# Attention with an expert layer behind it on one core: two count copies removed, a scale moved to VectorE, a subtraction to GpSimd, and one pair's V maxima at other places

## The chip, the core and the metric

The kernel runs on one core of a Trainium2 chip. The metric is the time of one execution in microseconds (us). The engines are TensorE (PE; its weight loads are PEld), VectorE (DVE), ScalarE (ACT), GpSimd (POOL) and SyncE (SP, which issues DMAs). Each engine works through its own instructions in the order in which they stand.

## What is computed

The inputs are q, k and v of 8 batches, 8 heads, 1152 positions and 64 columns. Pairs of neighbouring queries are averaged, so that there are 576 queries a head; attention follows, and the 4608 rows of 512 that come out go to the one of 8 experts that a router picks for each:

```python
q_pool = q.reshape(B, H, S // factor, factor, D).mean(axis=3)
attn = softmax(scale * q_pool @ k^T)
x = (attn @ v).transpose(0, 2, 1, 3).reshape(B * S, H * D)
e_idx = argmax(x @ w_gate)
...
h = relu(x[mask] @ w1[e]); ye = h @ w2[e]
out[mask] = gate_w[mask] * sigmoid(x @ w_output_gate)[mask, e] * ye
```

## The kernel before

**Attention** goes through 32 pairs (batch, two heads) in an order that is written out by hand. The program counts steps, 18 to a pair (one for each of 9 key blocks of each head) and 3 places to a step. In each step TensorE makes the scores of one block (L392 and L394, tile `sps`), one or two row maxima groups of the next pair (L329, tile `mp`), and sums of probabilities by V of a pair before (L421 to L423, tile `av`). VectorE takes the maxima (`pm`, L330). ScalarE makes two exponentials of a score block; the low part `pl` of the probabilities is their difference, made on VectorE where the block's number stands in `PLP` (L402, it reads the score's own PSUM buffer and sets it free) and on GpSimd for the others (L408). There are two score buffers, used in turn, so the scores of an odd block wait for L402 of the odd block before. When a head's sums are done, VectorE sets the `av` buffer free with three instructions (`r`, `r`, `xb`, L430 to L432).

**Preparation of a pair** is a table of places (`PREPF` for the first pair, `PREP0` for the second, `PREP` for the others): loads, casts, splits, and at the end V. V is scaled by a power of two from its largest absolute value: ScalarE makes the maxima (`amax`, L266, tiles `junk` and `am`), TensorE adds them up over the partitions (`gmax`, L271), VectorE cuts the exponent out of PSUM into `ex` (`scale` 0, L276), GpSimd clamps and multiplies `ex` to `inv` (`scale` 1, L279, 128 x 2 elements), VectorE takes the reciprocal `sc` (`scale` 2, L281). Then V's high half is made on ScalarE (`vh`, L284, tile `vt`) and its low half on GpSimd (`vs`, L288, and `vl`, L291). Inside attention TensorE, VectorE, ScalarE and GpSimd follow the written order.

**The router** behind each batch's last pair counts rows by expert in `cum` (bf16, L582) and scatters row numbers by DMAs that GpSimd issues (L587). Once, in the sixth batch, `setup` copies `cum` into `cb1` (L757) and adds it up over the partitions by a matmul (L761) to pick an early expert.

**The expert layer** (`run`) loads that expert's weights, splits the first one into a rounded half `w1h` on ScalarE (L865) and the rest `w1l` on VectorE (L866) while the last pair's attention still runs, and goes through tiles of 256 rows (`l1`, L901 to L911, `l2`, L923 to L925). Before the first tile `totals1` copies `cum` into `cb` (L940), a matmul adds it up into `cp` (L942), and `totals2` and `totals3` make the tables of tiles on VectorE (L947 to L1023).

Of the kernel before, what the change touches and what calls it, by code (L numbers as in the profile page):

```python
# [8 lines left out]
F32 = mybir.dt.float32  # L9
F32R = mybir.dt.float32r  # L10
F16 = mybir.dt.float16
BF16 = mybir.dt.bfloat16
# [3 lines left out]
ALU = mybir.AluOpType  # L16
# [8 lines left out]
        (53, 'lv'), (71, 'amax', 0), (74, 'amax', 1), (81, 'gmax'), (82, 'scale', 0), (85, 'scale', 1), (90, 'scale', 2), (93, 'vh', 0), (93, 'vs', 0), (96, 'vh', 1), (97, 'vl', 0), (100, 'vs', 1), (104, 'vl', 1))  # L25
PREPF = ((0, 'lf'), (1, 'fsel'), (3, 'qsv'), (4, 'kh', 0), (5, 'kh', 1), (6, 'klh', 0), (7, 'klh', 1), (8, 'sk', 0, 0), (9, 'sq0'), (10, 'sk', 0, 1), (11, 'sl', 0, 0), (13, 'qd'),
         (45, 'sl', 0, 1), (46, 'sk', 1, 0), (48, 'sk', 1, 1), (51, 'sq1'), (54, 'sl', 1, 0), (57, 'sl', 1, 1), (56, 'lv'),
         (78, 'amax', 0), (82, 'amax', 1), (88, 'gmax'), (89, 'scale', 0), (92, 'scale', 1), (95, 'scale', 2), (97, 'vh', 0), (97, 'vs', 0), (100, 'vh', 1), (101, 'vl', 0), (103, 'vs', 1), (107, 'vl', 1))
PREP = ((0, 'lk'), (12, 'kh', 0), (12, 'qsum'), (17, 'kh', 1), (18, 'kl'), (18, 'dk', 0), (19, 'dk', 1), (22, 'qh'), (24, 'dq', 0), (25, 'dq', 1), (26, 'ql'), (29, 'qd'), (30, 'dl', 0), (32, 'dl', 1),
        (63, 'lv'), (82, 'amax', 0), (88, 'amax', 1), (93, 'gmax'), (94, 'scale', 0), (95, 'scale', 1), (99, 'scale', 2), (100, 'vh', 0), (101, 'vs', 0), (103, 'vl', 0), (107, 'vh', 1), (107, 'vs', 1), (110, 'vl', 1))  # L30
BURST = {0: 2, 2: 2, 4: 2, 6: 2, 8: 1, 10: 2, 12: 2, 14: 2, 16: 3}
# [31 lines left out]


def attention(tc, qT, kT, vL, wg, keep, xrows, idscr, cum, pairs, setup, scat, init):
    nc = tc.nc
    nb = len(pairs) // 4
    with ExitStack() as ctx:
# [27 lines left out]
        def free(k):  # L96
            held.discard(k)
            banks.remove(k)
            banks.append(k)
# [5 lines left out]
        order = [(LASTN - 2) % 3, (LASTN - 1) % 3, LASTN % 3]  # L105
# [21 lines left out]
        def prep(n, table):  # L127
# [6 lines left out]
            kp = ld.tile([128, S], F32R, name=f"kp{n}", tag="kp", bufs=KPB)  # L134
# [9 lines left out]
            ex = sm.tile([128, 2], U32, name="ex")  # L144
            inv2 = sm.tile([128, 2], F32, name="inv2")
# [128 lines left out]
            def scale(i):  # L274
                if i == 0:
                    nc.vector.tensor_scalar(out=ex, in0=gm[0].bitcast(U32), scalar1=0x7F800000, scalar2=None, op0=ALU.bitwise_and)  # L276
                    free(gm[1])
                elif i == 1:
                    nc.gpsimd.tensor_scalar(out=inv2, in0=ex.bitcast(F32), scalar1=2.0 ** -100, scalar2=2.0 ** 3, op0=ALU.max, op1=ALU.mult)  # L279
                else:  # L280
                    nc.vector.reciprocal(out=sc, in_=inv2)  # L281

# [9 lines left out]

            P = functools.partial
            fns = dict(lf=lf, fsel=fsel, qsv=qsv, klh=klh, sk=sk, sl=sl, sq0=sq0, sq1=sq1, qd=qd, lk=lk, lv=lv, kh=kh, kl=kl, qsum=qsum, qh=qh, ql=ql, dk=dk, dq=dq, dl=dl, amax=amax, gmax=gmax, scale=scale, vh=vh, vs=vs, vl=vl)
            out = {}
            for r, name, *arg in table:
# [149 lines left out]
        ones = keep['ones']  # L446
# [57 lines left out]
        def router(b, xb):  # L504
# [90 lines left out]
            if b == max(nb - 3, 0):  # L595
                yield from setup(psum, free)
# [112 lines left out]
class Moe:  # L709
# [38 lines left out]
    def setup(self, psum, free):  # L748

        nc, kp, k, P1 = self.tc.nc, self.kp, self.keep, self.P1  # L750
        V = nc.vector
        if not P1:
            V.memset(k['oh1'], 0.0)
            V.memset(k['ef'][:, 0:2], 0.0)
            return
        cb = kp.tile([128, 8], BF16, name="cb1")
        V.tensor_copy(out=cb, in_=self.cum)  # L757
        yield
        yield 1
        cp, ck = psum(True)  # L760
        nc.tensor.matmul(cp[:, 0:8], lhsT=k['ones'], rhs=cb, start=True, stop=True)  # L761
        em = k['em8'][:, 0]
        cn, eq, mx, mi = cp[:, 0:8], cp[:, 8:16], cp[:, 16:17], cp[:, 17:18]
        V.tensor_reduce(out=mx, in_=cn, axis=AX.X, op=ALU.max)
        yield
        ms = kp.tile([128, 1], F32, name="mx1")
        V.tensor_copy(out=ms, in_=mx)
        V.tensor_tensor(out=eq, in0=cn, in1=ms.broadcast_to([128, 8]), op=ALU.is_equal)
        yield
        V.tensor_tensor(out=eq, in0=eq, in1=em, op=ALU.mult)  # L770
        V.tensor_reduce(out=mi, in_=eq, axis=AX.X, op=ALU.min)
        yield
        V.tensor_scalar(out=k['ef'][:, 1:2], in0=mi, scalar1=8.0, scalar2=None, op0=ALU.add)
        V.tensor_tensor(out=k['oh1'], in0=em, in1=mi.broadcast_to([128, 8]), op=ALU.is_equal)
        V.memset(k['ef'][:, 0:1], 0.0)
        yield
        V.tensor_scalar(out=k['es'], in0=mi, scalar1=8.0, scalar2=None, op0=ALU.add)
        ri = kp.tile([128, 2], U32, name="ri1")
        rb = cp[:, 18:19]
        V.tensor_scalar(out=rb, in0=mi, scalar1=8.0, scalar2=float(ESTRIDE), op0=ALU.add, op1=ALU.mult)  # L780
        V.tensor_tensor(out=ri, in0=k['Tp'][:, 0], in1=rb.broadcast_to([128, 2]), op=ALU.add)
        free(ck)
        yield
        self.gather_ids(-1, ri, kp, 1)
        for _ in range(8):
            yield
        self.gather(-1, kp, 1, self.early)

    def run(self):
        tc, k, P1, NT = self.tc, self.keep, self.P1, self.NT  # L790
        nc = tc.nc
        V = nc.vector
        with ExitStack() as ctx:
            def pool(name, bufs=1, **kw):
                return ctx.enter_context(tc.tile_pool(name=name, bufs=bufs, reuse_waits="tile", **kw))

            m1 = pool("m_1")
# [20 lines left out]
            W1 = [wp1.tile([128, 4, 1024], F32R, name=f"w1{x}") for x in "hl"]  # L818
# [41 lines left out]
                    c = nc.sync.value_load(z['chg'][0:1, t:t + 1], min_val=0, max_val=1)  # L860
                    lastw[0] = wload((t + 1) % 2, bass.ds(e, 1), cond=c, cond_hint=False, **kw)

            def split1(t, c):
                raw = raw1[(t + 1) % 2]
                nc.scalar.copy(out=W1[0][:, c], in_=raw[:, c])  # L865
                V.tensor_tensor(out=W1[1][:, c], in0=raw[:, c], in1=W1[0].bitcast(F32)[:, c], op=ALU.subtract)  # L866

            def split2(t, c):
                z = slice(2 * c, 2 * c + 2)
# [66 lines left out]
            z = {}  # L936

            def totals1():
                cb = m1.tile([128, 8], BF16, name="cb")
                V.tensor_copy(out=cb, in_=self.cum)  # L940
                cp = z['cp'] = ps_y.tile([128, 512], F32, name="cp", tag="yp")
                nc.tensor.matmul(cp[:, 0:8], lhsT=k['ones'], rhs=cb, start=True, stop=True)  # L942

            def totals2():
                cp = z['cp']
# [116 lines left out]
            order = list(range(-P1, NU))  # L1062

            def tile_(i, t, u):
# [19 lines left out]
                for c in range(4):  # L1084
                    if u is not None:
                        split1(u, c)
                    if acts:
                        acts.pop(0)()
# [10 lines left out]
            pend = []  # L1099
            E = mybir.EngineType  # L1100
            for c in range(4):
                split1(order[0], c)
            todo = [totals2, totals3, first]
            late = [totals2s]
            if P1:
                with tc.high_priority():
                    xt(order[0])
            else:
                totals1()
                while todo:  # L1110
                    todo.pop(0)()
                xt(order[0])
            with tc.manual_schedule(engines={E.PE, E.DVE, E.Activation}):
                if P1:
                    totals1()
                    while todo:
                        todo.pop(0)()
                for i, t in enumerate(order):
                    tile_(i, t, order[i + 1] if i + 1 < len(order) else None)
                while pend:  # L1120
                    pend.pop(0)()
            rv = nc.values_load(z['tot'][0:1, 0:1], min_val=0, max_val=NT + 8)  # L1122
            NL[0] = NU + len(rest)
            with tc.If(rv > 0):
                for t in range(NU, NL[0]):
                    gid(t)
                    gat(t)
                    e = nc.sync.value_load(z['er'][0:1, t - NU:t - NU + 1], min_val=0, max_val=7)
                    wload((t + 1) % 2, bass.ds(e, 1))
                    for c in range(4):  # L1130
                        split1(t, c)
                    xt(t)
                    for c in range(4 if halves(t) > 1 else 0):
                        split2(t, c)
                    for g in range(4):
                        l1(t, g)()
                    for j in range(halves(t)):
                        l2(t, j)()
# [58 lines left out]
```

## Time and profile before

| what | value |
|---|---|
| median of 3 runs | 1541.13 us (1538.14 to 1545.73) |
| the profiled execution | 1546.89 us, its span 1545.2 us |
| PE busy | 1486.4 us (96%) |
| PEld busy | 1347.8 us (87%) |
| DVE busy | 1111.8 us (72%) |
| ACT busy | 1123.6 us (73%) |
| POOL busy | 999.0 us (65%) |

The span is the time that the profile sees, and the 1.7 us around it belong to the execution's own time. Busy time is what an engine spent in instructions; matmuls overlap and their ends are modelled, so a PE that is busy all the time can still have waited in between for a short while. In a row of the timeline, the brackets at the end give the idle time of the engine ahead of that instruction and what ended it.

### The profile page before, as it was taken

How to read it: one execution, taken by the hardware profiler on the slowest of the kernel's cores; microseconds unless marked ns; L12 is line 12 of the kernel's file. 1: busy time of each engine (PE TensorE's matmuls, PEld its weight loads, DVE VectorE, ACT ScalarE, POOL GpSimd, SP SyncE). 2: the span in 40 equal slices, each digit the busy share in tenths (PEclk: the TensorE clock that was granted, in tenths of full speed). 3: DMA queues.
4: the chain of work that ended last, by engine and by line, in shares of the span. 5: the costliest groups of instructions: out<-in, count | busy, mean ns of one | idle time of the engine just before them, and what ended most of it. 6: DMA issues, size and time to landing. Idle time of an engine off the chain costs nothing. (4 is left out here: it accounts for less than half of the span.)

```text
span 1545.2 us, 40879 instructions
## 1 busy us (share of the span) xinstructions
PE 1486.4 (96%) x15838; PEld 1347.8 (87%) x15838; DVE 1111.8 (72%) x2315; ACT 1123.6 (73%) x1949; POOL 999.0 (65%) x915
## 2 busy tenths in 40 slices
PE   7999999999999999999999999969999999999996
PEld 6999999999999998999998899957888888888874
DVE  7677777777777777777777677658777777777762
ACT  5888888888888887888888788854565565565542
POOL 4887888788889888889888888726333333333200
PEclk9999999999999999999999999989999999999999
DMA  5477466665675576556756566055826656544550
GB/s 166 132 182 185 131 164 166 168 148 132 166 181 135 134 179 157 145 133 171 170 140 163 132 173 160 19 220 167 337 97 222 251 201 227 196 156 154 205 184 9
DMA packets 91983, 253.34 MB, mean 164 GB/s; under 512 B 12714, under 2 KB 16954, under 8 KB 91778
## 3 DMA queue, kind: packets, MB, share of 16 engines
q1 hardware_dynamic: 81194, 228.93, 52.5%
q0 software_dynamic: 9152, 20.85, 4.0%
q8 instruction: 129, 2.11, 0.6%
q10 hardware_dynamic: 1440, 0.89, 0.2%
q14 instruction: 68, 0.56, 0.1%
HBM read 164.23 MB, written 23.02 MB: 121 GB/s over the span
## 5 line engine op out<-in xcount | busy, mean ns | idle before, releaser
L330 DVE TENSOR_REDUCE pm<-mp 128x1 f32<-128x384 f32 x864 | 452.7, 550 | 214.2 <-PE mp L329 209.7
L408 POOL TENSOR_TENSOR pl<-p,ph 128x576 f16<-128x576 f32 x381 | 488.2, 1285 | 154.9 <-ACT ph L407 139.5
L406 ACT ACTIVATE p<-sps 128x576 f32<-128x576 f32 x381 | 248.8, 653 | 94.0 <-PE sps L394 57.3
L329 PE MATMUL mp<-ka,qa 128*128 128x384 f32 x960 | 315.4, 345 | 0.0
L421 PEld LDWEIGHTS <-ph 128*128 128x128 f16 x2880 | 262.4, 97 | 43.5 <-issue 29.6
L392 PE MATMUL sps<-qa,ka 128*128 128x288 f32 x1152 | 279.3, 324 | 19.1 <-DVE pl L402 10.3
L421 PE MATMUL av<-vt,ph 128*128 128x65 f16 x2880 | 295.1, 194 | 2.6 <-DVE xb L432 2.2
L422 PE MATMUL av<-vt,ph 128*128 128x64 f16 x2880 | 293.0, 194 | 0.0
L423 PE MATMUL av<-vt,pl 128*128 128x65 f16 x2880 | 292.2, 192 | 0.0
L422 PEld LDWEIGHTS <-ph 128*128 128x128 f16 x2880 | 265.2, 97 | 0.8
L423 PEld LDWEIGHTS <-pl 128*128 128x128 f16 x2880 | 265.5, 99 | 0.0
L329 PE MATMUL mp<-kb,qb 66*128 66x384 f32 x768 | 261.7, 341 | 0.6 <-DVE kb L203 0.6
L394 PE MATMUL sps<-qb,kb 68*128 68x288 f32 x1152 | 248.2, 298 | 0.0
L407 ACT ACTIVATE ph<-sps 128x576 f16<-128x576 f32 x381 | 247.4, 649 | 0.0
L901 PE MATMUL hps<-x,w1h 128*128 128x512 f32 (+1 forms) x704 | 231.4, 390 | 5.1 <-DVE x L885 2.8
L392 PEld LDWEIGHTS sps<-qa,ka 128*128 128x128 f32 x1152 | 184.9, 191 | 24.8 <-DVE pl L402 9.4
L394 PEld LDWEIGHTS sps<-qb,kb 68*128 68x128 f32 x1152 | 187.1, 191 | 0.0
L329 PEld LDWEIGHTS mp<-ka,qa 128*128 128x128 f32 x960 | 179.3, 191 | 1.3 <-DVE pm L330 1.0
L903 ACT COPY hs<-hps 128x512 f32<-128x512 f32 (+1 forms) x88 | 49.1, 557 | 171.5 <-PE hps L901 163.1
L901 PE MATMUL hps<-x,w1l 128*128 128x256 f32 (+1 forms) x704 | 165.8, 277 | 0.0
L398 ACT ACTIVATE ph<-sps 128x576 f16<-128x576 f32 x195 | 127.6, 655 | 51.1 <-PE sps L394 35.1
L402 DVE TENSOR_TENSOR pl<-sps,ph 128x576 f16<-128x576 f32 x195 | 146.6, 752 | 22.9 <-ACT sps L399 19.8
(232 smaller groups left out, 2944.9 us busy)
## 6 DMA issues: line engine op xcount, KB each, us to landing
ka<-xk SPq DMA_DIRECT2D x120, 288.0 KB
raw1b<-in_w_dram SPq DMA_DIRECT2D x24, 1024.0 KB
raw2b<-in_w_dram SPq DMA_DIRECT2D x24, 1024.0 KB
raw1a<-in_w_dram SPq DMA_DIRECT2D x22, 1024.0 KB
raw2a<-in_w_dram SPq DMA_DIRECT2D x22, 1024.0 KB
vp<-in_vL_dram SPq DMA_DIRECT2D x32, 576.0 KB
qp<-in_qT_dram SPq DMA_DIRECT2D x31, 576.0 KB
kpf<-in_kT_dram SPq DMA_DIRECT2D x31, 576.0 KB
```

Of the source, the lines that this page charges most:

```text
L329: nc.tensor.matmul(mp, lhsT=l, rhs=r, start=j == 0, stop=j == len(ops) - 1)
L330: nc.vector.tensor_reduce(out=pm[:, i:i + 1], in_=mp, axis=AX.X, op=ALU.max)
L392: nc.tensor.matmul(sps[:, j, 0:288], lhsT=ka[:, h, ks], rhs=qa[:, o + 288 * j:o + 288 * j + 288], start=True, stop=False)
L394: nc.tensor.matmul(sps[:, j, 0:288], lhsT=kb[:, h, ks], rhs=qb[:, h, 288 * j:288 * j + 288], start=False, stop=True)
L402: nc.vector.tensor_tensor(out=pl.rearrange("p (j n) -> p j n", j=2), in0=x, in1=ph2, op=ALU.subtract)
L406: nc.scalar.activation(out=p32.rearrange("p (j n) -> p j n", j=2), in_=x, func=AF.Exp, scale=1.0 / 16)
L407: nc.scalar.activation(out=ph2, in_=x, func=AF.Exp, scale=1.0 / 16)
L408: nc.gpsimd.tensor_tensor(out=pl, in0=p32, in1=ph, op=ALU.subtract)
L421: nc.tensor.matmul(av_[:, qb, 0:65], lhsT=hi, rhs=vt[:, h, c, 0:65], start=c == 0 and qb == 0, stop=False)
L422: nc.tensor.matmul(av_[:, qb, 0:64], lhsT=hi, rhs=vt[:, h, c, 66:130], start=False, stop=False)
L423: nc.tensor.matmul(av_[:, qb, 0:65], lhsT=lo, rhs=vt[:, h, c, 0:65], start=False, stop=c == NC - 1 and qb == 4)
L901: nc.tensor.matmul(hp[:, f, 0:n], lhsT=W1[l][:, c, fs], rhs=d['x'][:, c, 0:n], start=c == 0 and l == 0, stop=c == 3 and l == 0)
```

## The change

1. `cb1` and `cb` are gone: the two counting matmuls (L761, L942) read `cum` itself.
2. `scale` 1 (L279) of all 32 pairs is issued on VectorE instead of GpSimd.
3. The four subtractions `w1l` of the early expert (L866, in `split1`) are issued on GpSimd instead of VectorE; those of later tiles stay.
4. In `PREPF`, `gmax` goes from place 88 to 99, the three `scale` steps from 89, 92 and 95 to 100, `vh`, `vs` and `vl` by 6 places each.

```diff
 PREPF = (...
-         (78, 'amax', 0), (82, 'amax', 1), (88, 'gmax'), (89, 'scale', 0), (92, 'scale', 1), (95, 'scale', 2), (97, 'vh', 0), (97, 'vs', 0), (100, 'vh', 1), (101, 'vl', 0), (103, 'vs', 1), (107, 'vl', 1))
+         (78, 'amax', 0), (82, 'amax', 1), (99, 'gmax'), (100, 'scale', 0), (100, 'scale', 1), (100, 'scale', 2), (103, 'vh', 0), (103, 'vs', 0), (106, 'vh', 1), (107, 'vl', 0), (109, 'vs', 1), (113, 'vl', 1))
...
-                    nc.gpsimd.tensor_scalar(out=inv2, in0=ex.bitcast(F32), scalar1=2.0 ** -100, scalar2=2.0 ** 3, op0=ALU.max, op1=ALU.mult)
+                    nc.vector.tensor_scalar(out=inv2, in0=ex.bitcast(F32), scalar1=2.0 ** -100, scalar2=2.0 ** 3, op0=ALU.max, op1=ALU.mult)
...
-        cb = kp.tile([128, 8], BF16, name="cb1")
-        V.tensor_copy(out=cb, in_=self.cum)
...
-        nc.tensor.matmul(cp[:, 0:8], lhsT=k['ones'], rhs=cb, start=True, stop=True)
+        nc.tensor.matmul(cp[:, 0:8], lhsT=k['ones'], rhs=self.cum, start=True, stop=True)
...
-            def split1(t, c):
+            def split1(t, c, eng=V):
...
-                V.tensor_tensor(out=W1[1][:, c], in0=raw[:, c], in1=W1[0].bitcast(F32)[:, c], op=ALU.subtract)
+                eng.tensor_tensor(out=W1[1][:, c], in0=raw[:, c], in1=W1[0].bitcast(F32)[:, c], op=ALU.subtract)
...
-                cb = m1.tile([128, 8], BF16, name="cb")
-                V.tensor_copy(out=cb, in_=self.cum)
...
-                nc.tensor.matmul(cp[:, 0:8], lhsT=k['ones'], rhs=cb, start=True, stop=True)
+                nc.tensor.matmul(cp[:, 0:8], lhsT=k['ones'], rhs=self.cum, start=True, stop=True)
...
-                split1(order[0], c)
+                split1(order[0], c, nc.gpsimd)
```

VectorE in the 29th pair, where the V scale of one pair is made between other pairs' work; numbers behind names are buffers. Before:

```order
L330 TENSOR_REDUCE pm<-mp_19514 128x1
L276 TENSOR_SCALAR ex<-tp 128x2
L430 TENSOR_SCALAR r<-av_19206,sc 128x5
L431 RECIPROCAL r<-r 128x5
L432 TENSOR_TENSOR xb<-av_19206,r 128x5x64
L330 TENSOR_REDUCE pm<-mp_19548 128x1
L330 TENSOR_REDUCE pm<-mp_19552 128x1
L402 TENSOR_TENSOR pl<-sps_19541,ph 128x576
L281 RECIPROCAL sc<-inv_18306 128x2
```

The same place of the change:

```order
L330 TENSOR_REDUCE pm<-mp_19512 128x1
L276 TENSOR_SCALAR ex<-tp 128x2
L279 TENSOR_SCALAR inv_18306<-ex 128x2
L430 TENSOR_SCALAR r<-av_19204,sc 128x5
L431 RECIPROCAL r<-r 128x5
L432 TENSOR_TENSOR xb<-av_19204,r 128x5x64
L330 TENSOR_REDUCE pm<-mp_19546 128x1
L330 TENSOR_REDUCE pm<-mp_19550 128x1
L402 TENSOR_TENSOR pl<-sps_19539,ph 128x576
```

The new instruction stands directly behind the one whose result it reads, and ahead of the three that set the `av` buffer free; so it does from the sixth pair on, in 27 pairs. In pairs 2 to 5 one to three instructions stand between the two, and in the first pair the reciprocal follows at once.

ScalarE around the first pair's first score blocks (`sh` is the buffer of a shifted K, in the score buffers of PSUM). Before:

```order
L266 ACTIVATE junk,am<-vp 128x576
L197 CAST ka_122<-sh 128x576
L406 ACTIVATE p_442<-sps_437 128x576
L407 ACTIVATE ph<-sps_437 128x576
L284 ACTIVATE vt_138<-vp,sc 128x9x64
L123 DMA qb_127<-mr 1x4x128 x2
L398 ACTIVATE ph<-sps_462 128x576
L399 ACTIVATE sps_462<-sps_462 128x2x288
L284 ACTIVATE vt_138<-vp,sc 128x9x64
L406 ACTIVATE p_487<-sps_482 128x576
```

The same place of the change:

```order
L197 CAST ka_122<-sh 128x576
L406 ACTIVATE p_437<-sps_432 128x576
L407 ACTIVATE ph<-sps_432 128x576
L123 DMA qb_127<-mr 1x4x128 x2
L398 ACTIVATE ph<-sps_455 128x576
L399 ACTIVATE sps_455<-sps_455 128x2x288
L406 ACTIVATE p_483<-sps_478 128x576
L407 ACTIVATE ph<-sps_478 128x576
L284 ACTIVATE vt_138<-vp,sc 128x9x64
L398 ACTIVATE ph<-sps_508 128x576
```

V's two high halves stand behind the third and fourth score block instead of the first and second. On TensorE L271 goes with them, from ahead of five maxima groups and the first block's scores to behind the second block's.

GpSimd in the last pair, with the early expert's weight. Before:

```order
L408 TENSOR_TENSOR pl<-p_21752,ph 128x576
L408 TENSOR_TENSOR pl<-p_21803,ph 128x576
L408 TENSOR_TENSOR pl<-p_21875,ph 128x576
L408 TENSOR_TENSOR pl<-p_21932,ph 128x576
L408 TENSOR_TENSOR pl<-p_21990,ph 128x576
L408 TENSOR_TENSOR pl<-p_22046,ph 128x576
```

The same place of the change:

```order
L408 TENSOR_TENSOR pl<-p_21801,ph 128x576
L864 TENSOR_TENSOR w1l<-raw1a,w1h 128x1024
L408 TENSOR_TENSOR pl<-p_21873,ph 128x576
L864 TENSOR_TENSOR w1l<-raw1a,w1h 128x1024
L408 TENSOR_TENSOR pl<-p_21930,ph 128x576
L864 TENSOR_TENSOR w1l<-raw1a,w1h 128x1024
L408 TENSOR_TENSOR pl<-p_21988,ph 128x576
L864 TENSOR_TENSOR w1l<-raw1a,w1h 128x1024
```

On VectorE the same four are gone from ahead of four of the last pair's L402. ScalarE's four casts `w1h` stand where they stood.

## Rows read from the trace of the kernel before

**Rows 1.** Stretches: length, busy us (instructions) of PE, PEld, DVE, ACT, POOL; clock; DMA
```profile
30.00:40.00 10.00, 8.59 (x37) 7.82 (x36) 6.10 (x14) 6.75 (x12) 6.23 (x6) 0.67 0.48 143
...
100.00:1000.00 900.00, 885.68 (x11987) 834.73 (x11986) 665.45 (x1655) 758.21 (x1400) 763.09 (x686) 1.00 0.60 151
```

**Rows 2.** Lines L279 and L281: durations in ns min/median/max, first and last start
```profile
L279 POOL TENSOR_SCALAR inv<-ex x32: 227/233/248, 28.1 to 994.1; 128x2 f32<-128x2 f32 x32
L281 DVE RECIPROCAL sc<-inv x32: 152/155/158, 29.7 to 995.0; 128x2 f32<-128x2 f32 x32
```

**Rows 3.** Timeline of DVE and of POOL, 846 to 850 us: start, length, instruction
```profile
846.08 1.05 POOL L587 DMA_INDIRECT idscr<-tid,posi  x1 [0.16 <-issue]
846.63 3.11 DVE L757 COPY cb<-cum 128x8 bf16<-128x8 bf16 x1
847.16 2.54 POOL L408 TENSOR_TENSOR pl<-p,ph 128x576 f16<-128x576 f32 x2
```

**Rows 4.** Waits of 845 to 856 us: total, times, longest
```profile
PE av L421 <- DVE xb L432: 1.3, 1, 1.3
```

**Rows 5.** Timeline of DVE and POOL, the tables after attention
```profile
1048.62 1.03 POOL L587 DMA_INDIRECT idscr<-tid,posi  x1 [0.30 <-issue]
1049.32 0.34 DVE L1008 TENSOR_SCALAR efD<-efD 128x20 f32<-128x20 f32 x1
```

**Rows 6.** Timeline of the 29th pair's V scale, 899 to 903 us
```profile
899.81 0.14 DVE L276 TENSOR_SCALAR ex<-tp 128x2 uint32<-128x2 uint32 x1
...
899.92 1.28 POOL L408 TENSOR_TENSOR pl<-p,ph 128x576 f16<-128x576 f32 x1 [1.75 <-ACT ph L407]
...
901.68 0.75 DVE L402 TENSOR_TENSOR pl<-sps,ph 128x576 f16<-128x576 f32 x1
...
902.57 0.50 PE L392 MATMUL sps<-qa,ka 128*128 128x288 f32 x2
```

**Rows 7.** Timeline of the 7th and of the 31st pair's V scale
```profile
212.52 0.14 DVE L276 TENSOR_SCALAR ex<-tp 128x2 uint32<-128x2 uint32 x1
212.91 1.30 POOL L408 TENSOR_TENSOR pl<-p,ph 128x576 f16<-128x576 f32 x1
213.47 0.23 DVE L430 TENSOR_SCALAR r<-av,sc 128x5 f32<-128x5 f32 x1 [0.82 <-PE mp L329]
...
961.70 0.14 DVE L276 TENSOR_SCALAR ex<-tp 128x2 uint32<-128x2 uint32 x1
961.89 1.33 POOL L408 TENSOR_TENSOR pl<-p,ph 128x576 f16<-128x576 f32 x1
```

**Rows 8.** Timeline of the first pair's V maxima and first score blocks
```profile
27.27 0.63 ACT L197 CAST ka<-sh 128x576 fp32r<-128x576 f32 x1
27.42 0.38 PE L271 MATMUL tp<-am,onesf 128*128 128x2 f32 x2 [1.56 <-ACT junk L266]
...
29.96 0.68 PE L392 MATMUL sps<-qa,ka 128*128 128x288 f32 x2
...
36.05 0.50 PE L392 MATMUL sps<-qa,ka 128*128 128x288 f32 x2 [1.41 <-DVE pl L402]
```

**Rows 9.** Timeline of the last pair with the early weight
```profile
1020.37 1.48 DVE L866 TENSOR_TENSOR w1l<-raw1a,w1h 128x1024 fp32r<-128x1024 f32 x1 [1.16 <-ACT w1h L865]
1020.74 0.69 ACT L399 ACTIVATE sps<-sps 128x576 f32<-128x576 f32 x1
1021.78 0.74 DVE L402 TENSOR_TENSOR pl<-sps,ph 128x576 f16<-128x576 f32 x1
```

**Rows 10.** Groups by line on POOL to 1000 us: busy us, mean ns
```profile
L231 POOL TENSOR_TENSOR kp<-kpf,xk 128x1152 fp32r<-128x1152 f32 x31 | 82.4, 2658 | 0.0
```

**Rows 11.** Timeline of the tables' start and of the first tile
```profile
1044.29 0.18 DVE L940 COPY cb<-cum 128x8 bf16<-128x8 bf16 x1
...
1044.75 0.16 DVE L947 SCALAR_TENSOR_TENSOR ni<-oh,cp 128x8 int32<-128x8 f32 x1 [0.28 <-PE cp L942]
...
1058.14 0.50 PE L901 MATMUL hps<-x,w1h 128*128 128x512 f32 x1 [2.32 <-DVE hs L904]
```

## The prediction

> **What bounds the kernel now.** I read the busy times by stretch first, then the waits of TensorE, then the timeline at each place that the change touches. In the 900 us of attention TensorE is busy for 885.7 us at full clock, VectorE for 665 and GpSimd for 763 [rows 1]. So TensorE's own stream sets the time there, and VectorE and GpSimd have room on average. What counts is where TensorE waits in between. Such a place is the scores of an odd block: in the 29th pair VectorE frees the score buffer at 901.68 + 0.75 = 902.43 and the scores start at 902.57 [rows 6]. The 0.14 us between is the shortest distance that I find there, so TensorE had been waiting for VectorE. A delay of VectorE ahead of that instruction is then a delay of TensorE, and nothing later gives it back, because ScalarE and GpSimd in turn wait for TensorE. This decides how the edits are to be priced: not by an engine's load, but by whether the instruction stands ahead of a score buffer's release.
>
> **The counts' copies.** The copy into `cb1` looks like nothing, 128 x 8 elements of 2 bytes. It took 3.11 us, from 846.63 to 849.74 [rows 3]. GpSimd was issuing a scatter when it began and had two `pl` right behind it, which ended at 849.70, 0.04 us ahead of the copy. So the copy was held until GpSimd paused. It reads SBUF and writes SBUF; the neighbours on VectorE that were not held mostly read PSUM. Three instructions later comes `xb`, for which TensorE waited 1.3 us [rows 4]. Without the copy that goes: **-1.3 us**, between 0 (another wait ends there next) and -3.1 (the whole copy). The second copy, `cb`, is 0.18 us and `ni` starts 0.46 us after it began [rows 11]; VectorE is then busy without a gap down to the `hs` for which TensorE waits 2.32 us at 1058 [rows 11]. The matmul can now run while VectorE is still making x, so `ni` follows x at once: **-0.4 us**, between 0 and -0.5. TensorE's first tile itself doesn't start much earlier, since it needs x as well.
>
> **The scale on VectorE.** On GpSimd it took 0.233 us, and the reciprocal of the same size takes 0.155 us on VectorE [rows 2]. By these alone the move would put 32 x 0.155 = 5.0 us on VectorE and take 7.5 from GpSimd, which hides it. But this instruction also reads SBUF and writes SBUF, and it runs in the middle of GpSimd's subtractions, as the copy of rows 3 did. The nearest row of its own kind is a clamp of 20 fp32 elements: 0.34 us, ending at 1049.66 where a scatter on GpSimd ends at 1049.65 [rows 5], a good 0.15 us over the reciprocal. Against it, the reciprocal goes from SBUF to SBUF too and was never held, at most 158 ns in 32 places [rows 2]. I take it that clamps are held like copies.
>
> The trace tells how often. I went through all 27 pairs in which it stands directly behind `ex` and looked at what GpSimd does at the end of `ex`. In 11 of them an instruction of GpSimd is under way (the first and the last are the 7th and the 31st pair [rows 7], and the 29th is another [rows 6]); the time to the end of GpSimd's unbroken work is 1.2 to 1.5 us there, 1.31 on average, 14.4 together. In six of the 11 VectorE then waits anyway, for the end of a head's sums, 0.82 us in the 7th pair [rows 7], 0.75 on average: 4.5 us are hidden. In three the scores follow 0.7 us after the release instead of 0.14, which hides 1.7. So 8.2 us reach TensorE. In the other 16 the instruction itself stands ahead of the release; in 11 of these the scores follow at once, 11 x 0.155 = 1.7 us. That makes 9.9 us for 27 pairs; four earlier pairs at the same rate add 1.5: **+11.4 us**. The ends: 0, if it is not held and its 0.155 us are hidden, and 31 x 1.28 = 40 us, if it met a whole `pl` each time. I stay with the count, since it comes from the places themselves. GpSimd's own gain is worth nothing, as its `pl` mostly start when ScalarE is done [rows 6].
>
> A rule of the Trainium skill speaks against this edit as well: the page SBUF — State Buffer, section "Who interferes with whom", says that VectorE and GpSimd share a pair of ports, that copies, casts and `tensor_scalar` on VectorE may claim it, and that the later comer stands still until the other's instruction is over. Rows 3 agree that it stands still, but not for how long: by the page the copy would have run when the scatter ended, and it waited for two more instructions. By the page the cost would be at most one `pl` a place, 11 x 1.28 instead of 14.4, 0.3 us less in the sum.
>
> **The early weight on GpSimd.** GpSimd's subtraction of 1152 columns takes 2.66 us [rows 10], so one of 1024 takes about 2.4, four 9.5. ScalarE's cast sets it off. Three `pl` behind it start when ScalarE is done with their `ph`, later than that, and the fourth starts some 0.5 us later than now; the sums need it several steps after. So nobody waits for it. On VectorE the four go away. Only the last of them holds a release: ScalarE is done at 1021.43, and L402 starts at 1021.78 behind `w1l` [rows 9]; nearly all of these 0.35 us go: **-0.3 us**, between +0.5 (the late `pl`) and -1.2 (the four casts' slots all shortened). ScalarE's wait for the weight's DMA stays.
>
> **The first pair.** TensorE waits 1.56 us for `am` ahead of L271 [rows 8]. Now L271 stands behind the second block's scores, when `am` is long there. The five maxima groups behind it move up by about 1.5 us, and the first scores can start when ScalarE has cast the shifted K out of their buffer, 27.27 + 0.63 = 27.9 us, so at about 28.0 instead of 29.96: 1.9 us earlier [rows 8]. The fourth block's scores, now at 36.05 with another wait of 1.41 us, gain about 0.5 us more, because ScalarE no longer makes V's half ahead of the second block's exponentials. I take **-2.4 us**. The least is 0 (the wait comes back at V's halves). The most is -4.9: TensorE's clock in this stretch was granted at 0.67 [rows 1], between the levels of 1.2 and 2.4 GHz, and if the missing wait also kept it at 2.4 GHz, the third of 10 us that is lost comes on top of the 1.56.
>
> **The sum**: -1.3 - 0.4 + 11.4 - 0.3 - 2.4 = +7.0 us. Against the profiled execution of 1546.9 us that is 1553.9. That execution lies 5.8 us above the median of the runs, 1541.1, and the same difference against the median gives **1548.1 us**, 0.45% slower. About 0.5% (7.7 us) is what a measurement of this kernel can tell from no change.
>
> **Rivals.**
> - *The scale isn't held, no slower than before.* If an instruction of two elements with constants passes as the reciprocal does [rows 2], the +11.4 shrink to 0.155 us at about 22 places where scores follow at once, 3.4 us, or to nothing: the sum is -1.0 to -4.4, about 1538.5 us. It turns on this one form, which no row shows; for it the reciprocals, against it the 20-element clamp [rows 5] and the copy [rows 3]. Chance 0.2.
> - *It is held at nearly every place and longer.* A held VectorE shifts the next steps against GpSimd, and the copy of rows 3 shows that one hold can outlast three instructions. With 24 of 31 places at 1.31 us less the same share hidden (0.56) it costs 18 us, with the rest of the sum +14: 1555. With holds of two `pl` each it would be near 1575. Chance 0.17.
> - *The start gives more.* With the clock up from the first pair on, -4.9, and the scale free: 1534 to 1537. Chance 0.05. That the last edit does nothing, because the first scores' inputs come late, is inside the main case.
>
> **How the numbers follow.** The main case has 0.58, and its own range is +2 to +12 us, 1543 to 1553, by the ends of the start's gain and by three places more or fewer that are held. The range over all cases, 1536 to 1557, leaves out the far part of the second rival and the best of the third. Slower by over 0.5% (above 1548.8): somewhat under half of the main case, 0.26, and most of the second rival, 0.14: 0.4. Faster by over 0.5% (below 1533.4): the third rival at its best and a little of the first, 0.05. Within 0.5%: 0.55.
>
> **What would show it.** Line L279 on VectorE with a few durations near 0.15 us and about a third near 1.3 us, its long ones ending where a `pl` ends, means that I am right; all near 0.15 means the first rival. The wait for `xb` at 846 us is gone. TensorE's first scores start near 28 us. The four `w1l` on GpSimd last about 2.4 us each, and no `av` waits for the `pl` behind them. `ni` starts right behind x. I am wrong if L279 is never held, or if it is held and TensorE's stream runs on all the same.

## The result, and the profile after

The changed kernel took **1549.09 us** (median of 22 runs, 1542.34 to 1557.37) against 1542.62 for the kernel before in the same comparison (22 runs). The ratio is 1.0042, 95% interval 1.0028 to 1.0057: 6.5 us slower, within half a per cent. The forecast was +7.0.

The profiled executions differ by less: 1548.47 against 1546.89 us. The profile of before began late. Its first V maximum on ScalarE starts at 25.39 us; in the changed kernel the same instruction starts at 22.93, and in the runs below at 22.7 to 25.6 whatever the code, since it stands behind the loads. So below I measure programs from that instruction to the 32nd and last `ex` (the mask of V's maximum), which leaves the loads out. I call this the **length to the last mask**.

The stretches of the changed kernel (columns as in [rows 1]):

```profile
30.00:40.00 10.00, 9.04 (x48) 8.48 (x49) 5.23 (x9) 7.53 (x14) 7.46 (x7) 0.54 0.22 77
100.00:1000.00 900.00, 882.86 (x11918) 830.50 (x11917) 680.47 (x1676) 755.64 (x1394) 752.63 (x652) 1.00 0.59 151
```

TensorE does 2.8 us less in the 900 us than in [rows 1], VectorE 15.0 more. Where the 15.0 come from, the durations of the two lines of [rows 2] show (ns, min/median/max):

```profile
L279 DVE TENSOR_SCALAR inv<-ex x32: 156/171/1559, 28.8 to 993.0; 128x2 f32<-128x2 f32 x32
L281 DVE RECIPROCAL sc<-inv x32: 148/155/165, 29.0 to 995.5; 128x2 f32<-128x2 f32 x32
```

The median is a free instruction's, 171 ns; the longest takes nine times that. 12 of the 32 took over 1.2 us, one 0.49, the other 19 at most 0.22. These are two of the 12, on VectorE and GpSimd (start, length), and then one of the 19:

```profile
207.90 1.00 POOL L587 DMA_INDIRECT idscr<-tid,posi  x1 [0.16 <-issue]
208.70 1.56 DVE L279 TENSOR_SCALAR inv<-ex 128x2 f32<-128x2 f32 x1
208.91 1.31 POOL L408 TENSOR_TENSOR pl<-p,ph 128x576 f16<-128x576 f32 x1
...
301.55 1.28 POOL L408 TENSOR_TENSOR pl<-p,ph 128x576 f16<-128x576 f32 x1 [1.99 <-DVE pm L330]
301.60 1.25 DVE L279 TENSOR_SCALAR inv<-ex 128x2 f32<-128x2 f32 x1
...
271.22 0.17 DVE L279 TENSOR_SCALAR inv<-ex 128x2 f32<-128x2 f32 x1
...
271.89 1.29 POOL L408 TENSOR_TENSOR pl<-p,ph 128x576 f16<-128x576 f32 x1 [2.74 <-ACT ph L407]
```

At 301 the `pl` had begun 0.05 us ahead of the scale, and both end together, at 302.83 and 302.85. At 208, the longest, a scatter was under way with 0.20 us to go and a `pl` followed at once; the scale waited through both, to 210.26. At 271 the `pl` came 0.67 us later, and the scale was free. Behind the held instruction on VectorE stand `r` and `xb`, the end of a head's sums. TensorE's waits of 100 to 1000 us (total, times, longest) show who minds, and then one of the three waits of maxima groups:

```profile
PE sps L392 <- DVE sc L281: 5.4, 9, 0.6
PE av L421 <- DVE xb L432: 4.8, 9, 0.8
...
PE mp L329 <- DVE pm L330: 1.9, 3, 0.6
PE sps L392 <- ACT ph L407: 0.8, 2, 0.6
...
PE sps L392 <- DVE pl L402: 0.4, 1, 0.4
...
304.25 0.44 PE L329 MATMUL mp<-ka,qa 128*128 128x384 f32 x1 [0.63 <-DVE pm L330]
```

The same waits in the kernel before:

```profile
PE sps L392 <- DVE sc L281: 4.7, 8, 0.6
PE sps L392 <- ACT ph L407: 3.6, 4, 2.0
...
PE av L421 <- DVE xb L432: 2.2, 2, 1.3
```

There, the waits for `xb` came to 2.2 us in 2 places, 1.3 of them [rows 4] and thus the copy's, and no maxima group waited. In the changed kernel each of the 12 long scales is followed within 3 us by one such wait, nine for `xb` and three for the maxima, 6.7 us in all. The waits ahead of score blocks (L392, whatever ended them; L281 stands right behind an L402 on VectorE) did not grow: 8.3 us before, 6.6 now.

The start and the end, as [rows 8, 9, 11] for the kernel before:

```profile
22.93 0.69 ACT L266 ACTIVATE junk<-vp 128x576 f16<-128x576 f32 x1 [1.51 <-DVE pm L330]
...
25.63 0.42 PE L392 MATMUL sps<-qa,ka 128*128 128x288 f32 x2
...
27.41 0.28 PE L271 MATMUL tp<-am,onesf 128*128 128x2 f32 x2
...
30.95 0.58 PE L392 MATMUL sps<-qa,ka 128*128 128x288 f32 x1 [1.54 <-DVE pl L402]
...
849.61 0.23 DVE L430 TENSOR_SCALAR r<-av,sc 128x5 f32<-128x5 f32 x1 [0.39 <-PE av L423]
...
992.81 0.14 DVE L276 TENSOR_SCALAR ex<-tp 128x2 uint32<-128x2 uint32 x1
...
1021.40 2.36 POOL L864 TENSOR_TENSOR w1l<-raw1a,w1h 128x1024 fp32r<-128x1024 f32 x1
1021.41 0.69 ACT L399 ACTIVATE sps<-sps 128x576 f32<-128x576 f32 x1
...
1022.19 0.76 DVE L402 TENSOR_TENSOR pl<-sps,ph 128x576 f16<-128x576 f32 x1 [2.31 <-ACT sps L399]
...
1042.93 0.17 DVE L582 TENSOR_TENSOR cum<-tp,cum 128x8 bf16<-128x8 f32 x1
...
1044.57 0.15 DVE L943 SCALAR_TENSOR_TENSOR ni<-oh,cp 128x8 int32<-128x8 f32 x1
...
1057.83 0.50 PE L899 MATMUL hps<-x,w1h 128*128 128x512 f32 x1 [2.94 <-DVE hs L902]
```

L271 has no wait any more. At 849.61 it is VectorE that waits for TensorE's sums, where before the held copy ended at 849.74. L402 starts 0.09 us behind ScalarE instead of 0.35. `ni` follows the last `cum` by 1.64 us; before it was 1044.75 against a `cum` at 1042.65 (its row is below), 2.10.

For the lengths, the rows of the kernel before:

```profile
25.39 0.68 ACT L266 ACTIVATE junk<-vp 128x576 f16<-128x576 f32 x1 [1.51 <-DVE pm L330]
...
992.51 0.14 DVE L276 TENSOR_SCALAR ex<-tp 128x2 uint32<-128x2 uint32 x1
...
1042.65 0.17 DVE L582 TENSOR_TENSOR cum<-tp,cum 128x8 bf16<-128x8 f32 x1
```

That is 967.12 us, and 992.81 - 22.93 = 969.88 for the changed kernel.

### The profile page after: what moved, and what is told of

It reads as the page before. It is cut to its first block, busy times and chain, and to the rows that moved or that the text cites. A ratio compares the mean times of both kernels' runs of the same rounds, so it can differ in the third digit from the quotient of the medians.

```text
span 1546.6 us, 40938 instructions
## 1 busy us (share of the span) xinstructions
PE 1487.3 (96%) x15838; PEld 1346.4 (87%) x15838; DVE 1124.5 (73%) x2341; ACT 1124.6 (73%) x1949; POOL 1001.1 (65%) x887
## 5 line engine op out<-in xcount | busy, mean ns | idle before, releaser
L392 PE MATMUL sps<-qa,ka 128*128 128x288 f32 x1152 | 279.4, 324 | 17.7 <-DVE pl L402 10.6
L392 PEld LDWEIGHTS sps<-qa,ka 128*128 128x128 f32 x1152 | 184.7, 191 | 23.7 <-issue 9.8
L402 DVE TENSOR_TENSOR pl<-sps,ph 128x576 f16<-128x576 f32 x195 | 147.2, 755 | 30.4 <-ACT sps L399 27.2
```

What stands on the lines that cost most here:

```text
L392: nc.tensor.matmul(sps[:, j, 0:288], lhsT=ka[:, h, ks], rhs=qa[:, o + 288 * j:o + 288 * j + 288], start=True, stop=False)
L402: nc.vector.tensor_tensor(out=pl.rearrange("p (j n) -> p j n", j=2), in0=x, in1=ph2, op=ALU.subtract)
```

## The experiments

All ratios are to the kernel before, measured beside them on the same chip. The first four ran on one chip, the exchanged kinds and the later scale on a second (where the kernel before took 1539.32 us instead of 1546.64 to 1546.95), the rest on a third; lengths of the second chip are not compared with others. The record does not name the chip of the result above, where the kernel before took 1542.62 us, so the changed kernel's lengths stand beside those of the other chips with that reserve. My theory was that the scale's hold is the whole loss. The rivals were that another edit causes it, and that VectorE is held there by something other than where the scale's operands lie.

**The scale back on GpSimd.** The changed kernel with

```diff
-                    nc.vector.tensor_scalar(out=inv2, in0=ex.bitcast(F32), ...
+                    nc.gpsimd.tensor_scalar(out=inv2, in0=ex.bitcast(F32), ...
```

> The changed kernel with its doubled scale back on GpSimd; all else stays changed. Theory (the scale is held by GpSimd's subtractions, and this is the whole loss): the other edits are left alone with their gains, at the start 3.6 to 4.1 us by the trace and at the counts' copies 1.5 to 3, so 5 to 7 us under the kernel before, a ratio of 0.9955 to 0.997, and 11 to 13 us under the changed kernel; VectorE's reciprocals stay at 0.155 us. Rival 1 (the loss comes from another edit, such as the later places of V's maxima or the late pl behind the early weight): only the 3 us of 31 instructions on VectorE go, and it stays 2 to 4 us over the kernel before, 1.001 to 1.003.

Measured: 1542.75 us, ratio 0.9977 (0.9963 to 0.9992): 3.6 us faster than before. Between this and 1.0042 lie 0.65%, 10.0 us. The gain of the other edits is smaller than expected, but the sign is clear: without the scale's move the change is a gain. Its rows:

```profile
24.14 0.68 ACT L266 ACTIVATE junk<-vp 128x576 f16<-128x576 f32 x1 [1.51 <-DVE pm L330]
...
987.26 0.14 DVE L276 TENSOR_SCALAR ex<-tp 128x2 uint32<-128x2 uint32 x1
```

The length to the last mask is 963.12 us, 6.8 less than in the changed kernel.

**Only the scale moved.** The kernel before with this one line on `nc.vector`.

> The kernel before with only the doubled scale moved to VectorE. Theory (held): 10 to 13 us slower than before, a ratio of 1.0065 to 1.0085, with about a dozen durations of 1.2 to 1.6 us in this instruction, each ending where a subtraction of GpSimd ends. Rival 1 (the loss is another edit's): 0 to 3.4 us slower, under 1.0022.

Measured: 1553.57 us, ratio 1.0045 (1.0027 to 1.0064), 7.0 us slower: the one edit makes a loss of the size of the whole, under the 10 to 13 us that I expected. Nine durations are over 1.2 us, not a dozen. The length is 995.47 - 22.82 = 972.65 us:

```profile
22.82 0.68 ACT L266 ACTIVATE junk<-vp 128x576 f16<-128x576 f32 x1 [1.52 <-DVE pm L330]
...
995.47 0.14 DVE L276 TENSOR_SCALAR ex<-tp 128x2 uint32<-128x2 uint32 x1
```

**The scale read from PSUM.** Same engine, same order of instructions, same places; only the mask is written to PSUM, where the kernel's matmuls put their results, and read from there, instead of SBUF, where its other tiles lie:

```diff
-                g = g[:, 0:2]
-                nc.tensor.matmul(g, ...
+                g = g[:, 0:4]
+                nc.tensor.matmul(g[:, 0:2], ...
...
-                    nc.vector.tensor_scalar(out=ex, in0=gm[0].bitcast(U32), ...
-                    free(gm[1])
+                    nc.vector.tensor_scalar(out=gm[0][:, 2:4].bitcast(U32), in0=gm[0][:, 0:2].bitcast(U32), ...
                 elif i == 1:
-                    nc.vector.tensor_scalar(out=inv2, in0=ex.bitcast(F32), ...
+                    nc.vector.tensor_scalar(out=inv2, in0=gm[0][:, 2:4], ...
+                    free(gm[1])
```

> The changed kernel, but the masked exponent is kept in PSUM, so that the doubled scale on VectorE reads PSUM instead of SBUF; the order of the instructions is the same on every engine. Theory (VectorE is held because this form reads SBUF and writes SBUF beside GpSimd): all 32 durations under 0.25 us, 4 to 7 us under the kernel before, 0.9955 to 0.9975. Rival 2 (what holds it isn't its operands' place but that VectorE writes SBUF, or waits at this point for something else): a dozen durations of over 1.2 us stay, and the time stays near that of the changed kernel, 1.004.

Measured: 1542.63 us, ratio 0.9980 (0.9965 to 0.9996): 3.1 us faster than before, where I expected 4 to 7. The durations, and one place with its `pl`:

```profile
L278 DVE TENSOR_SCALAR inv<-tp x32: 149/159/161, 28.7 to 983.8; 128x2 f32<-128x2 f32 x32
...
297.68 1.28 POOL L408 TENSOR_TENSOR pl<-p,ph 128x576 f16<-128x576 f32 x1 [2.02 <-DVE pm L330]
297.73 0.16 DVE L278 TENSOR_SCALAR inv<-tp 128x2 f32<-128x2 f32 x1
```

The same collision as at 301.55 in the changed kernel, 0.05 us apart, and no hold. In this trace a `pl` with over 0.7 us left to run is under way at 10 of the 32 places, and none of the scales takes over 161 ns. This settles that for this instruction the operand's place decides, and that the move to VectorE as such is free.

**The old places of V's maxima.** The changed kernel with `PREPF` as before.

> The changed kernel with the first pair's V maxima at their earlier places. Theory: the 3.6 to 4.1 us that its trace shows as won by the third pair are lost again, 1552 to 1553.5, a ratio to the kernel before of 1.006 to 1.007; TensorE waits again near 27.4 us for the accumulated maxima. Rival (the gain of the start is given back later, since the granted clock or another wait takes it): the time stays within 1 us of the changed kernel, 1.0035 to 1.005.

Measured: 1552.39 us, ratio 1.0049 (1.0028 to 1.0071). That is 1 us behind the changed kernel and cannot be told from it or from the expectation. The length is 972.63 us, 2.7 more than the changed kernel's, but it doesn't show the old places' price either: the fifth mask comes 122.49 us after the first maximum, 0.8 us sooner than the changed kernel's 123.28, and the difference arises behind it, where the two programs are the same.

**Each other edit alone**, on the kernel before: the copies gone, the table, the early weight's subtractions on GpSimd.

```diff
-        cb = kp.tile([128, 8], BF16, name="cb1")
-        V.tensor_copy(out=cb, in_=self.cum)
-        nc.tensor.matmul(cp[:, 0:8], lhsT=k['ones'], rhs=cb, start=True, stop=True)
+        nc.tensor.matmul(cp[:, 0:8], lhsT=k['ones'], rhs=self.cum, start=True, stop=True)
...
-         (78, 'amax', 0), (82, 'amax', 1), (88, 'gmax'), (89, 'scale', 0), ...
+         (78, 'amax', 0), (82, 'amax', 1), (99, 'gmax'), (100, 'scale', 0), ...
...
-                split1(order[0], c)
+                split1(order[0], c, nc.gpsimd)
```

> The kernel before with only the two copies of the counts gone. Theory: -1.3 us from the block at 846 us and -0.4 from the table of tiles, so 1.7 us faster, and up to 3.2 if the whole 3.11 us of the copy reach TensorE (the changed kernel's trace shows some 2.7 won between the 27th and the 29th pair): a ratio of 0.998 to 0.999. Rival (the copy is hidden, what is won there in the changed kernel comes from elsewhere): 1.000, and the distance of the 27th and 29th pairs stays 66.3 us as before.

> The kernel before with only the first pair's V maxima at the later places. Theory: -2.4 us by the sum of the prediction, 3.6 to 4.1 by the changed kernel's trace, all of it kept to the end, so a ratio of 0.9974 to 0.9985; by the third pair's mask 3.5 us earlier than before. Rival (the start's gain comes from another edit or is given back): 0.9995 to 1.001.

> The kernel before with only the early weight's four subtractions on GpSimd. Theory: -0.3 us, which no comparison of the times can show: 0.999 to 1.001; the fourth VectorE subtraction from the score buffer starts at most 0.1 us behind ScalarE's second exponential there instead of 0.35. Rival (the pl behind them come late and TensorE waits for them, or VectorE is held by GpSimd's longer work): 1 to 3 us slower, 1.0007 to 1.002.

Measured: 0.9990 (0.9971 to 1.0010), 0.9998 (0.9983 to 1.0013) and 0.9985 (0.9968 to 1.0002). No one of them can be told from no change by its time, and the table's lies on its rival's side. Their lengths say more, together with two runs of the version that reads PSUM, one of them with the old table:

> The version that reads the doubled scale from PSUM, with the first pair's V maxima back at their earlier places: the two counts' edits and the early weight remain. By the traces so far the later places are worth about 1 us (the first scores come 1.9 us earlier, and at a clock of 0.67 to 0.78 about 1 of it is left by the fourth pair): 0.9982 to 0.9995 of the kernel before, 0.5 to 1.5 us behind the version with the later places. By the prediction's term of 2.4 us: 2 to 3 us behind it, 0.9995 to 1.0005.

> The version that reads the doubled scale from PSUM, all else as changed, beside the one with the old places on the same chip. If it beats the kernel before, 0.9965 to 0.999 again; if the 0.998 was the luck of that comparison, 0.9995 to 1.0005.

Measured: 1.0001 (0.9986 to 1.0015) with the old places, 0.9982 (0.9968 to 0.9997) with the later ones. The second repeats 0.9980 on another chip; two comparisons, neither of whose intervals holds 1, so **this version beats both kernels**. Between the two lie 2.9 us, what the prediction's term would give, but the table alone gave 0.3, and the intervals allow both.

Where the lengths differ shows in five runs of the same chip, from the first maximum on, in us between starts of masks (L276):

| run (clock in 30 to 40 us) | to the 5th | 5th to 27th | 27th to 28th | 28th to 29th | to the last |
|---|---|---|---|---|---|
| early weight alone (0.67) | 124.49 | 682.76 | 34.02 | 32.35 | 966.44 |
| table alone (0.64) | 123.60 | 682.65 | 33.79 | 32.27 | 964.98 |
| copies gone alone (1.00) | 121.27 | 683.05 | 32.33 | 33.29 | 962.69 |
| PSUM, old table (0.80) | 122.97 | 683.19 | 32.28 | 33.51 | 965.15 |
| PSUM, later places (0.63) | 123.19 | 681.77 | 32.27 | 33.00 | 963.37 |

The early weight's edit lies behind the last mask, and the table's ahead of the second. So the last two rows are the same program from the fifth mask on, and differ by 2.0 us there; differences of 1 to 2 us between two lengths, each from one execution, are not an edit's for certain. The later places are ahead by 0.9 us at the fifth mask in the first two rows and behind by 0.2 in the last two. The copy's gain is clear where the copy was: 1.5 to 1.7 us from the 27th to the 28th mask. By the 29th mask 0.7 to 1.2 of it are gone, and 0.3 to 1.1 are left (65.62 us with only the copies gone, against 66.29 in the kernel before). The wait of 1.35 us that the copy caused is gone, and a shorter one is new, some 3 us behind the 28th mask. First the kernel before, then the one with the copies gone:

```profile
850.67 0.20 PE L421 MATMUL av<-vt,ph 128*128 128x65 f16 x1 [1.35 <-DVE xb L432]
```

```profile
864.74 0.20 PE L421 MATMUL av<-vt,ph 128*128 128x65 f16 x1 [0.49 <-DVE xb L432]
```

With the early weight alone, the fourth L402 starts 0.09 us behind ScalarE (1018.14 against 1017.36 + 0.69 = 1018.05), 0.26 less than in [rows 9]:

```profile
1017.36 0.69 ACT L399 ACTIVATE sps<-sps 128x576 f32<-128x576 f32 x1
...
1018.14 0.76 DVE L402 TENSOR_TENSOR pl<-sps,ph 128x576 f16<-128x576 f32 x1 [2.31 <-ACT sps L399]
```

**Another form of the same scale.** The changed kernel with a second tensor:

```diff
-                    nc.vector.tensor_scalar(out=inv2, in0=ex.bitcast(F32), scalar1=2.0 ** -100, scalar2=2.0 ** 3, op0=ALU.max, op1=ALU.mult)
+                    nc.vector.scalar_tensor_tensor(out=inv2, in0=ex.bitcast(F32), scalar=2.0 ** -100, in1=keep['eight'], op0=ALU.max, op1=ALU.mult)
```

> The changed kernel with the doubled scale in another form on VectorE: scalar_tensor_tensor with a constant tile of eights as its second tensor, SBUF to SBUF as before, same result. Theory A (only copies and operations with one tensor are held by GpSimd): 32 durations under 0.25 us, 0.997 to 0.9985 as with the scale on GpSimd or read from PSUM. Theory B (anything that both reads and writes SBUF on VectorE is held, the reciprocal only escaped because it follows a held instruction): a dozen durations over 1.2 us stay and the time stays at that of the changed kernel, 1.004.

Measured: 1551.09 us, ratio 1.0029 (1.0009 to 1.0049), 12 durations over 1.2 us, length 996.95 - 22.76 = 974.19 us, 10.8 more than the PSUM version on the same chip. Theory A falls: an instruction with two tensors in SBUF is held the same.

```profile
L279 DVE SCALAR_TENSOR_TENSOR inv<-ex,eight x32: 149/163/1397, 28.7 to 997.1; 128x2 f32<-128x2 f32 x32
...
22.76 0.69 ACT L266 ACTIVATE junk<-vp 128x576 f16<-128x576 f32 x1 [1.51 <-DVE pm L330]
...
996.95 0.14 DVE L276 TENSOR_SCALAR ex<-tp 128x2 uint32<-128x2 uint32 x1
```

**The two kinds exchanged, and the scale later.**

```diff
-                    nc.vector.tensor_scalar(out=inv2, in0=ex.bitcast(F32), scalar1=2.0 ** -100, scalar2=2.0 ** 3, op0=ALU.max, op1=ALU.mult)
+                    nc.vector.reciprocal(out=inv2, in_=ex.bitcast(F32))
                 else:
-                    nc.vector.reciprocal(out=sc, in_=inv2)
+                    nc.vector.tensor_scalar(out=sc, in0=inv2, scalar1=2.0 ** 100, scalar2=2.0 ** -3, op0=ALU.min, op1=ALU.mult)
```

The later scale is the changed kernel with `scale` 1 at place 99 instead of 95 in `PREP`, directly ahead of the reciprocal.

> The changed kernel with the two instructions' kinds exchanged: the reciprocal stands where the doubled scale stood, and a clamp with a multiplication (tensor_scalar, SBUF to SBUF) where the reciprocal stood; same result, same order of instructions on every engine. Theory (the kind of instruction decides, and a reciprocal from SBUF is never held): 32 reciprocals of under 0.2 us at the old place of the scale, and at the old place of the reciprocal 5 to 12 clamps of over 0.4 us, since a subtraction of GpSimd is under way at some of these; the time lies between the scale read from PSUM and the changed kernel, 0.998 to 1.002. Rival (the place decides, whatever instruction stands there): about a dozen reciprocals of over 1.2 us and the time of the changed kernel, 1.003 to 1.0045.

> The changed kernel with the doubled scale four steps later, directly ahead of the reciprocal. The table also shifts a block of sums on TensorE by this, so the time is the weaker witness. Theory (what counts is only whether a subtraction of GpSimd is under way when it starts): in the trace with the scale on GpSimd a subtraction is under way at 5 or 6 of the 32 reciprocals, so 4 to 8 long durations instead of 12, and 0.999 to 1.0025 of the kernel before. Rival (the instruction is held through something of its own place): at the new place none or nearly all are long.

Measured: 1.0001 (0.9987 to 1.0015) and 1.0001 (0.9985 to 1.0018). The exchanged kinds:

```profile
L279 DVE RECIPROCAL inv<-ex x32: 153/166/168, 30.0 to 982.4; 128x2 f32<-128x2 f32 x32
...
L281 DVE TENSOR_SCALAR sc<-inv x32: 155/158/1151, 30.2 to 984.9; 128x2 f32<-128x2 f32 x32
...
301.74 1.28 POOL L408 TENSOR_TENSOR pl<-p,ph 128x576 f16<-128x576 f32 x1 [2.02 <-DVE pm L330]
301.79 0.17 DVE L279 RECIPROCAL inv<-ex 128x2 f32<-128x2 f32 x1
```

The reciprocal at the old place meets the `pl` as the scale did, 0.05 us behind its start, reads and writes SBUF as it did, and takes 0.17 us; so do all 32, of which 10 have a `pl` with over 0.7 us to run beside them. The `tensor_scalar` in the reciprocal's place was held twice, fewer than the 5 I expected at least, because `pl` is rarely under way there. With the scale moved later three are held, where I expected 4 to 8. Theory B, that anything from SBUF to SBUF is held, falls too: **the kind of instruction decides, together with its operands' place, and whether a `pl` of GpSimd is under way when it starts.** Two places of the changed kernel mark the edges. In the third pair a `pl` had begun 0.01 us ahead, and the scale took 0.16 us. And the issue of an indirect DMA on GpSimd held the scale only near its own end (208 and 961 us); with 0.57 us to go it did not:

```profile
868.10 1.01 POOL L732 DMA_INDIRECT ids<-idscr,ri  x1 [0.31 <-issue]
868.54 0.17 DVE L279 TENSOR_SCALAR inv<-ex 128x2 f32<-128x2 f32 x1
```

The Trainium skill's page SBUF — State Buffer, section "Who interferes with whom", draws a line of this kind: `tensor_scalar`, copies and casts can take the port pair shared with GpSimd, an instruction with two inputs in SBUF contends with GpSimd's reads, and one with a single SBUF input outside the two-port modes doesn't contend. The runs agree on the first two: 12 long of 32 with one input as `tensor_scalar`, 12 of 32 with two inputs. The third fits the reciprocal, 0 of 32, if that has no two-port mode, which no run here shows.

## Why the prediction was right, term by term

- **The scale on VectorE, +11.4: right in mechanism, some 1.4 to 4.4 too large.** The times give 10.0 us (changed kernel against the scale on GpSimd), 9.6 and 9.3 (against the two runs from PSUM), 7.3 (the second form against PSUM), 7.0 (the scale alone); the lengths 6.5 to 6.8 for the changed kernel (across chips), 10.8 for the second form. I counted 11 held places among the 27 later pairs; 12 came, 8 of them in pairs that I had counted, the 7th and the 31st among them, the 29th not. The 32 scales lasted 14.2 us longer than free ones, and I had 14.4 for those 27. Two additions were too much: the 1.7 us for the instruction's own 0.155 us where it is not held (the version that reads PSUM, free at all 32 places, is as fast as the scale on GpSimd: 0.9980 and 0.9982 against 0.9977), and the step from 27 pairs to 31 (of the first pairs one was held, 0.49 us). Without them the term is the 8.2 us of held time that I let reach TensorE, in the middle of what was measured; as the way there was another (next point), that is in part luck.
- **The way it reaches TensorE was wrong.** I argued from the release of a score buffer, and took the 0.14 us of [rows 6] for a wait of TensorE. It was none to speak of: TensorE began its last sum 0.12 us ahead of those scores,

```profile
902.45 0.19 PE L423 MATMUL av<-vt,pl 128*128 128x65 f16 x1
```

  Behind the held scale come `r` and `xb`, and the sums have one buffer; so the next `av` waits, 4.8 us in 9 places against 1.7 in 3 in the version that reads PSUM,

```profile
PE av L421 <- DVE xb L432: 1.7, 3, 0.9
```

  and the maxima groups, 1.9 us against none. That is 5.0 us more. The waits ahead of score blocks add 0.4 (6.6 us against 6.2). Through which waits the rest of the loss goes isn't settled.
- **The copies, -1.3 and -0.4: right at the place, not kept whole.** The block at 846 us gave 1.5 to 1.7 us by the next mask, and of that 0.3 to 1.1 was left one mask later; that nothing later gives a delay back, as I argued, doesn't hold here. The place where the copy had been held is now a wait of VectorE for TensorE. `ni` comes 2.10 - 1.64 = 0.46 us earlier behind the last counts. That the tables' 0.46 us reach the end isn't shown: TensorE still waits there, 2.94 us for `hs`.
- **The early weight, -0.3: right where it can be seen.** The subtractions last 2.36 us on GpSimd (I had 2.4), L402 comes 0.26 us earlier, and no wait of `av` for a late `pl` appears. Alone it gave 0.9985 with an interval of 0.9968 to 1.0002, which neither shows nor excludes more.
- **The first pair, -2.4: right at the first blocks, not shown at the end.** From the first maximum to the first scores it was 29.96 - 25.39 = 4.57 us and is 25.63 - 22.93 = 2.70, the 1.9 us earlier that I worked out; to the next block that waits for L402, 36.05 - 25.39 = 10.66 and now 8.02. At the fifth mask the later places were ahead by 0.9 us where they were the only edit, and behind by 0.2 in the PSUM version and by 0.8 in the changed kernel (each against the same version with the old places). The times of these three comparisons give 0.3, 2.9 and 1.1 us for the later places, with wide intervals. The term took the gain at the 36 us block as kept, and much of it goes again. The granted clock may have its part: in 30 to 40 us it was 0.63 against 0.80 in the PSUM version's two runs and 0.54 against 0.78 in the changed kernel's, between the levels of 1.2 and 2.4 GHz. That the later places bring it down isn't shown.
- **The sum.** The other edits together gave -3.6 us, 0.9977, where the sum had -4.4; the scale 7 to 10 where it had 11.4. The loss and the gains both came out smaller than their terms, so the sum, 10.0 - 3.6 = 6.4 by the first comparison, was met all the same; that the two errors cancel is luck.
- **The rivals.** "The scale isn't held" is what the PSUM version does, and its forecast, -1.0 to -4.4 us, holds it: -3.1 and -2.8. "Held at nearly every place" falls: 13 of 32. Holds over more than one instruction, as the copy of [rows 3] had, came only where a scatter stood ahead of a `pl`, at 208 us and by 0.02 us at 961, and added 0.2 us at most; a hold of two `pl` came nowhere. By the Trainium skill's page SBUF — State Buffer, section "Who interferes with whom", the later comer stands still for one instruction of the other. The place at 301 agrees, where the scale ended 0.02 us behind the `pl`; the one at 208 doesn't, where it waited through two.

## What to carry to other kernels

A two-element instruction is not free because it is small. Before moving work from GpSimd to VectorE, look whether its inputs lie in SBUF, which kind of instruction it is, and what GpSimd does at the moment it starts; reading the value from PSUM, or another kind such as the reciprocal, keeps the move without the hold. When single edits are worth a tenth of a per cent, compare lengths inside the trace that start behind the loads, in runs of one chip, since the whole time scatters more than the edit; and compare them at several marks, since a gain at one can be gone at the next, and the same program differed by 2.0 us over 840.

## What the runs showed that I had not expected

- **How evenly a collision repeats.** Of the 12 long scales of the changed kernel, ten began 0.02 to 0.06 us behind the start of a `pl`, such as 301.60 behind 301.55. The order of work brings both to the same instant, so a place is mostly all or nothing. Which places are held changes with the program: the 29th pair's was held in the second form and free in the changed kernel.
- **The clock of the first 40 us isn't fixed by the instructions.** The kernel with only the copies gone and the one with only the early weight moved have the same instructions up to there and ran on one chip. Their granted clocks in 30 to 40 us were 1.00 and 0.67:

```profile
30.00:40.00 10.00, 7.46 (x48) 6.56 (x46) 6.97 (x16) 8.38 (x14) 7.30 (x7) 1.00 0.45 135
```

```profile
30.00:40.00 10.00, 8.53 (x37) 7.95 (x35) 5.59 (x11) 6.89 (x12) 7.82 (x8) 0.67 0.30 100
```

  The fifth mask came 121.27 us after the first maximum in the one and 124.49 in the other: 3.2 us, more than any edit but the scale is worth. What sets the clock there wasn't tried.
